# Paired attention heads on half of TensorE's rows and columns, in an attention and MLP kernel

## The chip, the cores and the metric

The kernel runs on one core of a Trainium2 chip. The metric is the device time of one execution in microseconds (us). Three runs of the kernel before took 725.65, 725.9 and 726.43 us; the median is 725.9. TensorE (PE in the profile) multiplies, VectorE (DVE), ScalarE (ACT) and GpSimd (POOL) work element by element, and SyncE (SP) issues most of the DMAs. TensorE reads its two operands from SBUF: a stationary one, which a weight load (PEld) brings into the array, and a moving one that streams through it. It writes to PSUM, which has eight banks.

## The reference

Attention with a sliding window and sink columns feeds a two-layer network with the gate h cos(h):

```python
scores = q @ k.T / sqrt(64)               # 4 batches, 8 heads, 768 positions, 64 per head
keep   = (pos_k < n_sink) | (0 <= pos_q - pos_k < window)      # n_sink 4, window 128
a      = softmax(where(keep, scores, -1e9))
x      = (a @ v), heads side by side      # 3072 tokens x 512
h      = x @ w_in                         # 512 x 2048
out    = (h * cos(h)) @ w_out             # 2048 x 512
```

The weights arrive as 64-bit floats and the result is float32. Most products are formed from numbers split into a rounded high part and a rest: high by high, high by rest, rest by high.

## The kernel before

The tokens are cut into 12 chunks of 256 (two 128-row blocks, CB = 2). Chunks 0 to 3 are the first 256 positions of the four batches; their heads are called early (`o.early`). The other eight chunks hold the late heads, whose queries see a band of one block and the sink columns. There are 8 heads in a chunk, so 32 early and 64 late heads, and `g` counts them.

An early head works in plain float32, which TensorE runs as two passes (two matmul records for each product). Query and key of two heads are loaded side by side and transposed on TensorE (`pe_turn`, L950), so that head 0 lies on rows 0 to 63 and head 1 on rows 64 to 127. `q_out` (L961) copies the query out of PSUM in two 64-row copies into `env.tqe`, where the other 64 rows of each head's 256 columns are zero; the key is copied whole. `scores_pe` (L987) is then one product over all 128 rows per head and query block, in which the zeros remove the other head. Likewise `load_v` (L921) puts a head's values beside 64 columns of zeros, and `values_pe` (L1204) forms one product per key block over all 128 columns, so that the second head of a pair adds to the bank of the first.

A late head splits query and key. The query of a pair is loaded and transposed once; each head has its rounded part and its rest stacked on the two row halves of one tile (`q_hi`, `q_lo`, L1004 and L1011). Each head loads its key twice, once on each row half (`load_k`, L908), transposes it on VectorE (`k_turn`), appends the sink columns, rounds it (`k_hi`) and subtracts (`k_lo`). `scores` (L1042) is two products of 264 columns per query block over 128 rows. VectorE merges the two halves of the window (`pick`), adds the mask and takes the minimum (`mask`); ScalarE takes the exponential; the probabilities are normalised, transposed on TensorE (`turn`), split, and `values` (L1220) forms seven products per head.

The dense work goes by pairs of chunks (512 tokens): six pairs of 16 slots. A slot is 12 products for h (`h_pair`, L476) and 12 for the output (`out_pair`, L523), each 128x128 by 512 columns. Dense pair 0 (chunks 0 and 1) runs beside the heads of chunks 2 and 3 and of the first late chunk, and so on; the last pair has no heads beside it. PSUM is shared out by name: in the late part four banks hold the outputs, two hold h, and attention has the two banks "s" and "tp".

The order on each engine is fixed when the kernel is built. `Plan.add` takes each step with its engines, an estimated duration, what it needs and a priority; `Plan.order` runs the list through a small model of the engines and emits the steps in the order in which they start there. The table `C` holds the offsets of these priorities. A step with several engines goes to one of them; `sub` offers POOL or DVE for subtractions. A step that issues DMAs is on SP's queue. `fill` (L1552) adds products that compute nothing, at the lowest priority, for moments when TensorE would wait in the model. `setup` (L233) comes ahead of the planned steps: it loads n_sink, window and the first two weight pieces (512 KB each) from ACT's queue. The first query and key loads are planned steps on SP's queue.

Of the kernel before, what the change touches and what calls it, by code (L numbers as in the profile page):

```python
# [31 lines left out]
    "POOLF": 0.999, "POOLPEN": 2.492, "R": 2, "RAW": 2, "SAME": 0.056, "SEM": 0.352, "SPE": -0.019, "STEP": 7.601,  # L32
# [140 lines left out]
def attn_moe_kernel(ctx, tc, q, k, v, n_sink, window, w_in, w_out, out):  # L173
# [59 lines left out]
    def setup():  # L233

        nc.scalar.dma_start(out=nw_i[:, 0, :], in_=n_sink.unsqueeze(0))
        nc.scalar.dma_start(out=nw_i[:, 1, :], in_=window.unsqueeze(0))
        nc.gpsimd.memset(ident, 0.0)
# [8 lines left out]
        for raw, src in env.first:  # L246
            nc.scalar.dma_start(out=raw.rearrange("p n w -> p (n w)"), in_=src)
# [104 lines left out]
    def x_minus(y, p, cs):  # L352
        def fn(e):
            nc.tensor.matmul(
                out=y.f(p, cs), lhsT=minus, rhs=xhi[:, p, cs], start=False, stop=True, skip_group_check=True
            )
        return fn

    def x_lo(y, p, cs, early):
        def fn(e):  # L360
            if early:
                copy(e, xlo[:, p, cs], y.f(p, cs))
            else:
                e.tensor_tensor(out=xlo[:, p, cs], in0=y.f(p, cs), in1=f32(xhi)[:, p, cs], op=ALU.subtract)
        return fn
# [195 lines left out]
    def sub(n):  # L561
        return (("POOL", 0.16 + n * 2.08e-3), ("DVE", dve(n)))
# [257 lines left out]
    def banded_path(ctx2):  # L820
# [634 lines left out]
        def after_softmax(g, o):  # L1455
# [76 lines left out]
            if o.sj:  # L1532
                oe = o.lead
                deps += oe.sinks
# [346 lines left out]
```

## Time and profile before

| | |
|---|---|
| median of three runs | 725.9 us (725.65 to 726.43) |
| profiled execution | 727.14 us, of which the span is 725.3 |
| PE busy | 707.8 us (98%) |
| PEld busy | 583.6 us (80%) |
| DVE busy | 599.3 us (83%) |
| ACT busy | 527.3 us (73%) |
| POOL busy | 127.0 us (18%) |
| granted TensorE clock, mean | 0.998 of full speed |
| DMA | 77.11 MB, mean 106 GB/s |

The span runs from the first to the last instruction of the core. Matmuls are pipelined and the profile models their ends, so records of neighbouring products overlap, and the time that a product costs is the distance to the start of the next. A wait is put down to whatever ended it last.

### The profile page before, as it was taken

How to read it: one execution, taken by the hardware profiler on the slowest of the kernel's cores; microseconds unless marked ns; L12 is line 12 of the kernel's file. 1: busy time of each engine (PE TensorE's matmuls, PEld its weight loads, DVE VectorE, ACT ScalarE, POOL GpSimd, SP SyncE). 2: the span in 40 equal slices, each digit the busy share in tenths (PEclk: the TensorE clock that was granted, in tenths of full speed). 3: DMA queues.
4: the chain of work that ended last, by engine and by line, in shares of the span. 5: the costliest groups of instructions: out<-in, count | busy, mean ns of one | idle time of the engine just before them, and what ended most of it. 6: DMA issues, size and time to landing. Idle time of an engine off the chain costs nothing.

```text
span 725.3 us, 12983 instructions
## 1 busy us (share of the span) xinstructions
PE 707.8 (98%) x3674; PEld 583.6 (80%) x3674; DVE 599.3 (83%) x1850; ACT 527.3 (73%) x1344; POOL 127.0 (18%) x213
## 2 busy tenths in 40 slices
PE   7888999999999999999999999999999999999997
PEld 6766787888888888888888888888888888888885
DVE  6889999998988978988978989888988875567763
ACT  3796886787797697796686886877887856566652
POOL 1010000000333222232231232232122322100000
PEclk9999999999999999999999999999999999999999
DMA  5665565533255333355433254533244410375651
GB/s 144 177 181 162 140 178 148 155 67 66 63 118 130 86 67 54 64 125 128 93 58 59 42 144 101 122 63 62 44 124 107 111 35 12 96 198 158 167 138 63
DMA packets 236500, 77.11 MB, mean 106 GB/s; under 512 B 221060, under 2 KB 221060, under 8 KB 236420
## 3 DMA queue, kind: packets, MB, share of 16 engines
q1 hardware_dynamic: 236128, 75.15, 43.5%
q10 hardware_dynamic: 292, 1.05, 0.5%
q8 instruction: 31, 0.51, 0.3%
q14 instruction: 49, 0.40, 0.2%
HBM read 69.86 MB, written 6.29 MB: 105 GB/s over the span
## 4 chain that ended last, share of the span: by engine, by line
PE 78%; ACT 12%; DVE 5%; issue 2%; DMA 2%; SPq 0%; ACTq 0%; DVEq 0%
PE h L476 30%; PE acc L523 30%; PE av L1239 4%; PE s L1048 4%; ACT p L1079 3%; PE s L992 2%; PE tp L1160 2%; PE av L1215 2%; DMA xk<-in_k_dram 2%; ACT p L1097 1%; ACT L485 1%; ACT L1079 1%; PE qk L955 1%; PE tp L1170 1%; ACT early L390 1%
## 5 line engine op out<-in xcount | busy, mean ns | idle before, releaser
L523 PE MATMUL acc<-whi_out,ghi 128*128 128x512 f32 x376 | 158.7, 422 | 0.0
L476 PE MATMUL h<-xhi,whi_in 128*128 128x512 f32 x384 | 155.3, 405 | 0.0
L476 PE MATMUL h<-xlo,whi_in 128*128 128x512 f32 x384 | 150.9, 393 | 0.0
L476 PE MATMUL h<-xhi,wlo_in 128*128 128x512 f32 x384 | 150.1, 391 | 0.0
L523 PE MATMUL acc<-whi_out,glo 128*128 128x512 f32 x376 | 147.8, 393 | 0.0
L523 PE MATMUL acc<-wlo_out,ghi 128*128 128x512 f32 x376 | 147.1, 391 | 0.0
L1198 POOL TENSOR_SCALAR_AFFINE_SELECT ph<-ph 128x512 fp32r<-128x512 f32 x128 | 87.2, 681 | 230.9 <-DVE ph L1191 227.1
L485 ACT ACTIVATE r<-h 128x512 f32<-128x512 f32 x96 | 57.1, 598 | 47.9 <-PE h L476 45.3
L476 PEld LDWEIGHTS h<-xlo,whi_in 128*128 128x128 f32 x384 | 72.1, 188 | 16.2
L523 PEld LDWEIGHTS acc<-whi_out,glo 128*128 128x128 f32 x376 | 70.6, 188 | 15.8
L476 PEld LDWEIGHTS h<-xhi,whi_in 128*128 128x128 f32 x384 | 72.3, 188 | 12.0 <-DVE r L498 0.3
L476 PEld LDWEIGHTS h<-xhi,wlo_in 128*128 128x128 f32 x384 | 72.5, 189 | 11.3
L523 PEld LDWEIGHTS acc<-whi_out,ghi 128*128 128x128 f32 x376 | 71.4, 190 | 10.4
L1079 ACT ACTIVATE p<-p,st 128x136 f32<-128x136 f32 (+1 forms) x192 | 79.3, 415 | 0.3
L523 PEld LDWEIGHTS acc<-wlo_out,ghi 128*128 128x128 f32 x376 | 71.3, 190 | 9.2
L498 DVE SCALAR_TENSOR_TENSOR r<-r,h 128x512 f32<-128x512 f32 x96 | 64.5, 674 | 16.9 <-ACT r L491 16.3
L507 ACT CAST ghi<-r 128x512 fp32r<-128x512 f32 x94 | 58.2, 619 | 19.6 <-PE acc L523 12.7
L514 DVE TENSOR_TENSOR glo<-r,ghi 128x512 fp32r<-128x512 f32 x94 | 65.3, 694 | 5.6 <-ACT ghi L507 4.9
L1070 DVE CUSTOM_DVE_ANT_0 p<-s,mk 128x136 f32<-128x136 f32 (+1 forms) x192 | 59.7, 313 | 6.2 <-PE s L992 2.8
L1008 ACT CAST l<-tq 64x256 fp32r<-64x256 f32 x64 | 25.8, 403 | 46.9 <-PE s L1048 46.4
L1056 DVE COPY_PREDICATED s<-mk,s 128x128 f32<-128x128 int32 x128 | 37.2, 291 | 25.6 <-PE s L1048 23.7
L1048 PEld LDWEIGHTS s<-r,l 128*128 128x128 f32 x256 | 46.4, 188 | 12.3 <-DVE ph L1191 1.4
(161 smaller groups left out, 1314.7 us busy)
## 6 DMA issues: line engine op xcount, KB each, us to landing
xk<-in_k_dram SPq DMA_DIRECT2D x256, 48.0 KB
raw<-in_moe_w_out_dram SPq DMA_DIRECT2D x16, 512.0 KB
wt<-in_moe_w_in_dram SPq DMA_DIRECT2D x32, 256.0 KB
raw<-in_moe_w_in_dram SPq DMA_DIRECT2D x14, 512.0 KB
v<-in_v_dram SPq DMA_DIRECT2D x64, 96.0 KB
raw<-in_v_dram SPq DMA_DIRECT2D x32, 192.0 KB
out_dram<-wt SPq DMA_DIRECT2D x22, 256.0 KB
wt<-in_moe_w_out_dram SPq DMA_DIRECT2D x20, 256.0 KB
```

Of the source, the lines that this page charges most:

```text
L476: nc.tensor.matmul(out=o.h, lhsT=w[:, c, fs], rhs=xx[:, c, :], start=(c == 0 and n == 0), stop=(c == NC - 1 and n == 2),)
L485: nc.scalar.activation(out=o.r, in_=o.h, func=AF.Sin, scale=0.5)
L498: nc.vector.scalar_tensor_tensor(out=o.r, in0=o.r, scalar=0.5, in1=o.h, op0=ALU.subtract, op1=ALU.mult)
L507: nc.scalar.copy(out=o.ghi, in_=o.r)
L514: e.tensor_tensor(out=o.glo, in0=o.r, in1=f32(o.ghi), op=ALU.subtract)
L523: nc.tensor.matmul(out=y.acc[j], lhsT=gg[:, j * P : (j + 1) * P], rhs=w[:, f, :], start=(f == 0 and n == 0), stop=(f == NFT - 1 and n == 2),)
L1048: nc.tensor.matmul(out=o.s_ps[j][:, :w], lhsT=o.l[:, j * P : (j + 1) * P], rhs=r.rearrange("p n s -> p (n s)")[:, c0 : c0 + w], start=(n = ...
L1056: nc.vector.copy_predicated(out=o.s_ps[j][:, :P], mask=below.bitcast(I32), data=o.s_ps[j][:, SW : SW + P])
L1070: nc.vector.tensor_tensor_reduce(out=o.pj[j][:, :w], in0=o.s_ps[j][:, :w], in1=masks[min(o.i0 + j, 2)][:, :w], op0=ALU.add, op1=ALU.min, s ...
L1079: nc.scalar.activation(out=o.pj[j][:, :w], in_=o.pj[j][:, :w], func=AF.Exp, bias=o.lead.st[:, 0, o.nth, j : j + 1], scale=-1.0, accum_out= ...
L1198: nc.gpsimd.affine_select(out=ph[:, :, b, :], in_=f32(ph)[:, :, 1, :], pattern=[[0, 2 * CB], [(-1, 1)[b], P]], compare_op=(ALU.is_gt, ALU. ...
L1239: nc.tensor.matmul(out=dst, lhsT=lhs, rhs=rhs, start=(n == 0), stop=(n == len(seq) - 1), skip_group_check=True)
```

## The change

Late heads are prepared in pairs. Key of head 0 is loaded on rows 0 to 63 and of head 1 on rows 64 to 127, query likewise; one rounding and one subtraction then serve both heads, for query and for key. `scores_two` forms the scores of both heads for one query block: for each head three products on its 64 rows (rounded by rounded, query rest by rounded key, rounded query by key rest), the two heads in turn, into banks "s" and "tp". `after_softmax` of the heads ahead is placed between the two score calls.

Early heads are prepared in pairs as well: no zeros, one copy of the query, scores as products on 64 rows, values as products of 64 columns into the two partition halves of one bank. The split of x after the early heads loses its product with the negated identity (`x_minus`), and its subtraction is on DVE. Query and key tiles of the early heads are double-buffered.

The first query and key loads move into `setup`: n_sink and the query on SP's queue, window and the key on ACT's queue, then one weight piece on each. The last output tile is copied in one step on ACT instead of two halves on ACT and DVE. `sub` no longer offers POOL for more than 256 columns. There are 110 fillers in place of 60 and 3 warming steps in place of 5, and the other numbers of `C` change.

```diff
-    "DV": 0.57, "DX": 4.638, "FILL": 60, "CV": 1.947, "CL": 15.777, "HO": -18.522, "SX": -5.15, "CR": 9.813,
+    "DV": -6.352, "DX": -1.287, "FILL": 110, "CV": 12.468, "CL": 26.528, "HO": -19.975, "SX": -6.773, "CR": 9.41,
-    "T": 6.724, "TH": 7.177, "WARM": 5, "WARM2": 0, "P0": 12.442, "A0": -3.102, "D0": 9.766, "G0": 3.059,
+    "T": 6.626, "TH": 6.919, "WARM": 3, "WARM2": 0, "P0": 9.866, "A0": 2.375, "D0": 8.59, "G0": -7.384, "S0": -8.12,
...
-        nc.scalar.dma_start(out=nw_i[:, 0, :], in_=n_sink.unsqueeze(0))
+        nc.sync.dma_start(out=nw_i[:, 0, :], in_=n_sink.unsqueeze(0))
         nc.scalar.dma_start(out=nw_i[:, 1, :], in_=window.unsqueeze(0))
+        for e, load in zip((nc.sync, nc.scalar), env.boot):
+            load(e)
...
-        for raw, src in env.first:
-            nc.scalar.dma_start(out=raw.rearrange("p n w -> p (n w)"), in_=src)
+        for e, (raw, src) in zip((nc.scalar, nc.sync), env.first):
+            e.dma_start(out=raw.rearrange("p n w -> p (n w)"), in_=src)
...
-        m = add([("PE", 0.12)], x_minus(y, p, cs), [i], t + 0.3)
-        env.minus.users.append(m)
-        j = add([("ACT", act(NT, False)), ("DVE", dve(NT))], x_lo(y, p, cs, True), [m], t + 0.6)
+        j = add([("DVE", dve(NT))], x_lo(y, p, cs), [i], t + 0.6)
...
-        return (("POOL", 0.16 + n * 2.08e-3), ("DVE", dve(n)))
+        return (("POOL", 0.16 + n * 2.08e-3), ("DVE", dve(n)))[n > NT :]
...
-            elif j < NJ - 1:
+            else:
                 i = [add(c[:1], out_scaled(y, j, other), d, c0 + 10.0)]
-            else:
-                i = [add([(e, w / 2)], out_half(y, j, n), d, c0 + 10.0) for n, (e, w) in enumerate(c)]
...
         def load_k(o):
-                for dup in range(2):
+                for h in range(2):
                     for c in range(2):
                         nc.sync.dma_start(
-                            out=o.xk[dup * 64 + c * 32 : dup * 64 + c * 32 + 32],
-                            in_=k[o.b, o.h, o.kb0 * P : (o.kb0 + o.nkb) * P, c * 32 : c * 32 + 32].rearrange(
+                            out=o.xk[h * 64 + c * 32 : h * 64 + c * 32 + 32],
+                            in_=k[o.b, o.h + h, o.kb0 * P : (o.kb0 + o.nkb) * P, c * 32 : c * 32 + 32].rearrange(
...
-        def q_out(o, odd):
-                r = slice(odd * 64, odd * 64 + 64)
-                copy(e, env.tqe[r, odd], o.qk[r, 0])
+        def q_out(o):
+                o.tq = env.tqe[o.btq.nth]
+                copy(e, o.tq, o.qk[:, 0])
...
+        def scores_pe(pair):
+                for j in range(CB):
+                    for o in pair:
+                        r = slice(o.odd * 64, o.odd * 64 + 64)
+                        c0 = max(o.i0 + j - 1 - o.kb0, 0) * o.sw
+                        nc.tensor.matmul(
+                            out=o.s_ps[j], lhsT=oe.tq[r, j * P : (j + 1) * P],
+                            rhs=oe.tk.rearrange("p n s -> p (n s)")[r, c0 : c0 + o.ws[j]], start=True, stop=True,
+                        )
...
+        def q_hi(o):
+                nc.scalar.copy(out=o.l, in_=o.tq)
+        def q_lo(o):
+                nc.vector.tensor_tensor(out=o.ql, in0=o.tq, in1=f32(o.l), op=ALU.subtract)
...
+        def scores_two(pair, j):
+                w, c0 = oe.ws[j], max(oe.i0 + j - 1 - oe.kb0, 0) * oe.sw
+                for o in pair:
+                    o.s_ps[j] = ps.tile([P, BW], F32, name=f"s_{o.tag}_{j}", tag=("s", "tp")[o.odd])
+                for n, (l, r) in enumerate(((oe.l, oe.r1), (oe.ql, oe.r1), (oe.l, oe.r2))):
+                    for o in pair:
+                        rows = slice(o.odd * 64, o.odd * 64 + 64)
+                        nc.tensor.matmul(
+                            out=o.s_ps[j][:, :w], lhsT=l[rows, j * P : (j + 1) * P],
+                            rhs=r.rearrange("p n s -> p (n s)")[rows, c0 : c0 + w], start=(n == 0), stop=(n == 2),
+                        )
...
+        def values_pair(pair, x):
+                av = x.f[oe.pair] = ps.tile([P, NT], F32, name=f"av_{oe.tag}", tag=oe.av_tag)
+                for n, (kb, qs) in enumerate(oe.cols):
+                    for o in pair:
+                        nc.tensor.matmul(
+                            out=av[o.odd * 64 : o.odd * 64 + 64, (qs[0] - oe.i0) * P : (qs[-1] + 1 - oe.i0) * P],
+                            lhsT=oe.v32[:, kb - oe.kb0, o.odd], rhs=o.pt[:, oe.offs[n] * P : oe.offs[n + 1] * P],
+                            start=(n == 0), stop=(n == len(oe.cols) - 1), skip_group_check=True,
+                        )
...
+        def score_two(g, j):
+            bss = [buf(tag, 1) for tag in ("s", "tp")]
+            c0 = add([("PE", 0.36)], scores_two(pair, j), [*oe.kr, *bss], te - 5 * T + C["DS"] + (3.25, 5.55)[j])
...
+            for n, w in enumerate(pair):
+                c1 = add([("DVE", dve(P) + 0.02)], pick(w, j), [c0], te - 5 * T + C["DS"] + (3.4, 5.7)[j] + 0.5 * n)
+                c2 = add(
+                    [("DVE", dve(w.w[j]) + 0.02)], mask(w, j),
...
+            else:
+                for j in range(CB):
+                    if behind and behind[0][1].comb:
+                        after_softmax(*behind.pop(0), (g, j))
+                    else:
+                        score_two(g, j)
```

## Rows read from the trace of the kernel before

**Rows 1.** The page's part 1, whole span: busy us, share, instructions.

```profile
PE 707.8 (98%) x3674; PEld 583.6 (80%) x3674; DVE 599.3 (83%) x1850; ACT 527.3 (73%) x1344; POOL 127.0 (18%) x213
```

**Rows 2.** Busy us by stretch: length, PE, PEld, DVE, ACT, POOL, clock, DMA.

```profile
0.00:57.00 57.00, 47.81 (x273) 39.31 (x274) 45.30 (x162) 38.95 (x129) 5.94 (x17) 1.00 0.62 165
20.00:57.00 37.00, 32.30 (x187) 24.98 (x187) 31.04 (x108) 33.05 (x113) 3.43 (x4) 1.00 0.65 171
57.00:190.00 133.00, 130.79 (x651) 105.41 (x652) 122.78 (x341) 101.34 (x248) 5.19 (x11) 1.00 0.49 124
190.00:640.00 450.00, 448.75 (x2396) 373.61 (x2395) 377.61 (x1215) 341.13 (x879) 115.84 (x186) 1.00 0.39 86
```

**Rows 3.** PE's groups by shape, whole span: busy us, mean ns, idle before.

```profile
L1239 PE MATMUL av<-ph,vr 128*64 128x128 f32 x128 | 28.8, 225 | 0.0
...
L1239 PE MATMUL av<-ph,vr 128*64 128x256 f32 x64 | 18.0, 281 | 0.0
...
L1556 PE MATMUL idle<-gt 128*128 128x256 f32 x60 | 13.1, 345 | 0.0
```

**Rows 4.** PE in order of time, late stretch: start us, us, instruction, count.

```profile
250.05 0.28 PE L1239 MATMUL av<-ph,vr 128*128 128x256 f32 x1
...
250.64 0.44 PE L523 MATMUL acc<-whi_out,ghi 128*128 128x512 f32 x1
250.92 0.40 PE L523 MATMUL acc<-wlo_out,ghi 128*128 128x512 f32 x1
...
260.56 0.41 PE L1048 MATMUL s<-r,l 128*128 128x264 f32 x2
260.80 0.39 PE L476 MATMUL h<-xhi,whi_in 128*128 128x512 f32 x1
```

**Rows 5.** PE in order of time, early heads beside dense products.

```profile
95.19 0.38 PE L992 MATMUL s<-tk,early 128*128 128x128 f32 x2
95.41 0.82 PE L1215 MATMUL av<-early,vpe 128*128 128x256 f32 x4
...
96.30 0.40 PE L476 MATMUL h<-xhi,wlo_in 128*128 128x512 f32 x1
96.53 0.39 PE L476 MATMUL h<-xlo,whi_in 128*128 128x512 f32 x1
...
97.45 0.59 PE L992 MATMUL s<-tk,early 128*128 128x256 f32 x2
97.88 0.38 PE L1170 MATMUL tp<-ident,p 128*128 128x128 f32 x2
```

**Rows 6.** DVE's groups by shape, 190 to 640 us.

```profile
L1039 DVE TENSOR_TENSOR r<-tk,r 128x408 fp32r<-128x408 f32 x57 | 34.0, 597 | 0.5
...
L1021 DVE STREAM_TRANSPOSE tk<-xk 128x384 f32<-128x384 f32 x57 | 32.1, 562 | 0.2
...
L1015 DVE TENSOR_TENSOR l<-tq,l 64x256 fp32r<-64x256 f32 x57 | 23.9, 420 | 1.5
```

**Rows 7.** The chain of waits, 0 to 70 us: start us, us, what.

```profile
2.32 5.88 DMA xk<-in_k_dram
...
8.34 0.66 PE qk L955 x2
```

**Rows 8.** All engines in order of time, the start.

```profile
4.70 0.69 PE L955 MATMUL qk<-ident,xq 128*128 128x128 f32 x2 [0.25 <-DVE neg L269]
```

**Rows 9.** Groups by line, 0 to 57 us.

```profile
L390 ACT COPY early<-qk 64x256 f32<-64x256 f32 x12 | 4.4, 366 | 12.2 <-PE qk L955 11.9
```

**Rows 10.** PE in order of time, the first dense product.

```profile
57.08 0.48 PE L476 MATMUL h<-xhi,whi_in 128*128 128x512 f32 x1
```

**Rows 11.** All engines in order of time, the end.

```profile
719.16 0.60 ACT L533 ACTIVATE raw<-acc 128x512 f32<-128x512 f32 x1 [0.76 <-PE acc L523]
...
720.51 0.38 ACT L543 ACTIVATE raw<-acc 128x256 f32<-128x256 f32 x1 [0.76 <-PE acc L523]
721.01 0.42 DVE L545 TENSOR_SCALAR raw<-acc 128x256 f32<-128x256 f32 x1 [6.60 <-ACT raw L543]
```

More of the change, by code (lines that the diff above doesn't have):

```diff
@@ L1025, in fn @@
             def fn(e):
-                sk = first.ts[:, o.h].unsqueeze(1).broadcast_to([P, o.nkb, NSINK])
-                copy(e, o.tk[:, :, P:], sk)
+                for h in range(2):
+                    r = slice(h * 64, h * 64 + 64)
+                    copy(e, o.tk[r, :, P:], first.ts[r, o.h + h].unsqueeze(1).broadcast_to([64, o.nkb, NSINK]))
             return fn
@@ L1362, in before_softmax @@
-                    i = add(dma(2), load_natural(xk_t, src, o.nkb), [bx], pk, lat=2.4 if g else 1.9)
+                        [("ACT", act(NT, False)), ("DVE", dve(NT))], q_out(o), [i, o.btq] + (early[:2] if g == 0 else []),
+                        t - 6 * T + C["EQ"] + 0.6,
+                    )
+                    bb.users.append(q0)
+                    bx, o.btk = buf("xk", 1), buf("tke", 2)
+                    src = lambda c: k[o.b, o.h + c, o.kb0 * P : (o.kb0 + o.nkb) * P, :]
+                    load = load_natural(xk_t, src, o.nkb)
@@ L1439, in softmax @@
+            for n, (_, o) in enumerate(group):
+                o.nm = [
+                    add(
+                        [("ACT", act(o.w[j]) + (0.0 if o.early else 0.19))], expo(o, j), ready, t + 1.02 * n + 0.01 * j,
+                        table="exp",
+                    )
+                    for j in range(CB)
+                ]
+                ex += o.nm
             t += 1.02 * (len(group) - 1) + 0.5
@@ new lines, in after_softmax @@
+            if o.early:
+                if o.odd == 0:
+                    return
+                pair = oe, _ = heads[g - 1], o
+                te = head_time(g - 1)
+                oe.bxv, bpt = buf("ve", 2), buf("phi", 1)
+                hold = [early[2:], [early_end]][g // 2] if g < 4 else []
+                v0 = add(dma(2), load_v_pair(oe), [oe.bxv, *hold], te - 2 * T + C["EV"] + 3.2, lat=2.4)
+                ready = [v0]
+                for m, w in enumerate(pair):
+                    pt = buf(w.tp_tag, 1)
+                    p0 = add([("PE", 0.107 * o.n)], turn_early(w), w.nm + [pt], head_time(g - 1 + m) + C["EA"] + 1.3)
+                    w.bp.users.append(p0)
+                    both = [("ACT", act(o.n * P, False)), ("DVE", dve(o.n * P))]
+                    p1 = add(both, p_out(w), [p0, ready[1] if m else bpt], head_time(g - 1 + m) + C["EA"] + 1.8)
+                    pt.users.append(p1)
+                    ready.append(p1)
+                bav = buf(oe.av_tag, 1)
+                y0 = add([("PE", 0.84)], values_pair(pair, x), [*ready, bav], te + C["EA"] + 5.0)
+                for bb in (oe.bxv, bpt, *early[2:]):
+                    bb.users.append(y0)
@@ L1640, in banded_path @@
             waiting.append((g, o))
-            if behind:
-                after_softmax(*behind.pop(0))
+            if o.early:
+                if behind and o.odd:
+                    for _ in range(2):
+                        after_softmax(*behind.pop(0))
+            elif o.odd == 0:
+                while behind and behind[0][1].early and len(behind) > 2 - g % 4:
+                    after_softmax(*behind.pop(0))
+            else:
+                for j in range(CB):
+                    if behind and behind[0][1].comb:
+                        after_softmax(*behind.pop(0), (g, j))
+                    else:
+                        score_two(g, j)
             if len(waiting) == o.nq:
```

361 lines of the change are left out of this document (140 added, 221 removed), and 11 rows, old and new, of the table C.

## The prediction

> **What bounds the kernel now.** I read the totals first, then the stretches, then the order of work on TensorE inside two stretches, and last the chain at the start and the end. The totals show PE busy 98% of the span, DVE 83%, ACT 73% [rows 1]. A busy PE counts the pipeline's latency too, so the share alone proves little. The stretches do: from 57 to 190 us and from 190 to 640 us PE has 130.79 of 133 and 448.75 of 450 us, at a granted clock of 1.00 (the 2.4 GHz level) throughout, while DVE falls from 122.78 of 133 to 377.61 of 450 [rows 2]. So after about 60 us the time is PE's list of products, and an instruction taken off that list is taken off the span, as long as DVE (92% in 57 to 190 us) keeps up. Before 57 us PE is not full (47.81 of 57, and 60 of its products there are fillers that compute nothing, 13.1 us [rows 2, 3]): this is a chain that runs through DMA, PE, ACT and DVE in turn, with ACT at 33.05 and DVE at 31.04 of the 37 us from 20 to 57 [rows 2].
>
> What a product costs is read from starts, not durations, since a dense 128x512 product is recorded as 0.40 us and the next one starts 0.23 to 0.24 us later [rows 4, 5]. A late score (one head, one 128-query block, two products of 264 columns) takes 260.80 - 260.56 = 0.24 us. A late value block of seven products takes from 250.05 to the second dense product after it, 250.92, less one dense step of 0.23, so 0.64 us [rows 4]. In the early heads a score of 128 columns takes 95.41 - 95.19 = 0.22 us, one of 256 takes 97.88 - 97.45 = 0.43, and the values of one head take 96.30 - 95.41 less 0.23 = 0.66 us [rows 5]. An early pair of heads so costs PE 2 x (0.22 + 0.43 + 0.66) = 2.62 us in scores and values; its transposes are the same before and after.
>
> **The change, part by part.** The sum is made against the profiled execution, 727.1 us (725.3 of span and 1.8 around it). That is 1.2 above the median of 725.9, which I take off at the end.
>
> *Late scores.* Per pair of heads and query block two calls of 0.24 us go (0.48), and one call comes with six products of 264 columns on 64 rows each, ordered low rows, high rows, low, high. The trace has no product on half of the rows, so I bound it. One product of 264 columns takes 0.12. If the two row halves run side by side completely, the call is three steps, 0.36; if not at all, six steps, 0.72. There are 32 pairs x 2 blocks = 64 calls, so the term lies between 64 x (0.36 - 0.48) = -7.7 and 64 x (0.72 - 0.48) = +15.4 us. I take 0.40, a third of a step above the low end, because each step must now hide two weight loads where the score row hides one per 0.12 us: 64 x -0.08 = -5.1 us. All 64 calls lie in the stretches where PE is full, so this counts whole.
>
> The Trainium skill, TensorE: Matmul & The Clock Gate, Part 3, gives 3.07 times for four row tiles and 2.38 times for three column tiles, some 78% of ideal; an estimate for two tiles by that page is 1.56 times, 0.46 us a call, and this term would be -1.3 us. No row here tests it.
>
> *Early pairs.* Scores become four products on row halves, values become products of 64 columns into the two halves of one bank. Complete overlap halves 2.62 us: -1.31 a pair; no overlap: 0. The weight loads have more time here (0.11 us for 128 columns of each of the two passes, [rows 5]), so I take -1.31 on PE. Eight of the 16 pairs (chunks 2 and 3) run beside the first dense pair, mostly in 57 to 190 us: -10.5 us if nothing else binds. DVE has 122.78 of 133 us there [rows 2]. Squeezed by 10.5 that would be 100%, so DVE has to lose work too. It does: a late pair loses one key transpose, one key rest and one query rest (0.562, 0.597 and 0.420 us [rows 6]), and of these operations 57 of the 64 that 64 heads need fall in 190 to 640 us, so seven, 3.5 pairs, are prepared before 190: 5.5 us, and merged copies give about one more. About 116 of 122.5 us is 95%, tighter than the 92% of now; I give back 2 us for that: -8.5.
>
> *The prologue.* The other eight pairs run before 57 us. There the first key transposes start at 8.34 us, released by a key load that took 5.88 us [rows 7], beside the two weight loads that ACT's queue issues at the start. Query and key now go out ahead of the weights, key on ACT's queue behind one tiny load, query on SP's behind the other; one weight load follows each. On SP the first value loads wait behind two small issues and one weight issue, and the first values are needed only after a whole softmax. PE took the query at 4.70 us [rows 8]; if the key is there once those two transposes are done, at about 5.0, 3.3 us go. Bounds: 0 (the masks or the weights are late next) to -3.6 (both at 4.70). I take -3.3. Per pair, at least the second of two 64-partition copies goes, 0.37 us of ACT or DVE time [rows 9], and at most PE's 1.31: between -3.0 and -10.5 us over eight pairs. Since the chain passes through all engines and ACT and DVE are at 89% and 84% from 20 to 57 us [rows 2], I take -4.0. The extra fillers, 50 of 256 columns, some 0.12 us each by the score row, come last in priority; at worst each stands once before needed work, +6 us; I take 0, because they run where PE would wait.
>
> *Late preparation.* Key load, transpose, rounding, rest, and query rounding and rest are now once a pair. In 190 to 640 us that takes (34.0 + 32.1 + 23.9) / 2 = 45 us from DVE [rows 6], and ACT loses the roundings. Neither is the bound there, so 0 on the span; it lowers the risk of PE waiting. Half of the key DMAs go as well; the queues were hidden. What is added is a wait: a paired score needs both attention banks, and behind it on PE stand dense products. A call holds each bank for PE's 0.4 and some four DVE steps of 0.3, about 2 us, and with values and transposes a bank is held for about 8 us of a pair's 14 to 15, so I cost it at 0; if each call waited 0.1 us it would be 6.4.
>
> *The end.* The last copy was halved over ACT and DVE, but the DVE half began only at 721.01, after ACT's 720.51 + 0.38; together 0.92 us. One ACT copy of 512 columns took 0.60 [rows 11]: -0.3.
>
> Sum: -5.1 - 8.5 - 3.3 - 4.0 - 0.3 = -21.2; 727.1 - 21.2 = 705.9, and 704.7 on the median's footing. I say 705.
>
> **Rivals.** *First, the tile change drains TensorE (slower).* A product's record outlasts its step by 0.40 - 0.23 = 0.17 us; if PE empties whenever it goes from whole-array to half-array products and back, every call pays up to 0.34. That is 64 late calls, +21.8, and 16 early calls in the full stretch, +5.4, and in the prologue perhaps +2: 705 + 29 = 734. It decides from 21 / 160 = 0.13 us per change. Against it: the late value block has three products of 64 columns among four of 128, and its 0.64 us is what 1280 streamed columns take at the dense rate of 512 per 0.23, plus 0.06 [rows 3, 4]. So if 64-column products are a mode of their own, a change costs next to nothing; if they are not, the row says nothing.
>
> The Trainium skill, TensorEngine Tiling (Array Packing), Key Properties, says that changing the tiling mode drains the engine; this is that rival, and the value block, as far as it goes, does not agree.
>
> *Second, the halves do not overlap (slower).* Late +15.4, early 0, start -3.3, copies -1, end -0.3: 737. For it: no row shows two products on the array at once. Against it: nothing in the operands forbids it, as the halves write separate banks or separate partitions.
>
> *Third, the order loses what PE gains.* DVE or the shared banks become the bound from 57 us on; only the start, half of the late term and a third of the early term stay: -3.3 - 2.5 - 3.5 = -9, so 717. For it: DVE's 92% in 57 to 190 us. Against it: the work that DVE loses.
>
> **How the numbers follow.** The forecast has 0.66, with its own range of 693 to 712 (late term at -7.7 and prologue at -10.5 below; early term and prologue at half above). The lossy order has 0.12 (712 to 723), the drain 0.12 (centred on 734, but reaching down to 715 at smaller prices), no overlap 0.10. A range of 692 to 724 leaves out no overlap, most of the drain and little else, about 2 in 10. Within 0.2% means within 1.5 us, about what a measurement can tell from no change: 0.03. Slower takes no overlap and some of the drain: 0.15. Faster 0.82.
>
> **What would show it.** Right: pairs of half-row products whose starts lie a few ns apart, and a late call of 0.36 to 0.45 us from its first product to the next dense one; early scores and values of a pair in 0.65 us each; the first key transpose near 5 us; the first dense product before 52 us instead of 57.08 [rows 10]; PE still 98% full after it. Wrong: products of the six starting 0.11 us apart one by one (no overlap); a gap of over 0.1 us ahead of the first half-row product or the first dense one behind it (drain); DVE at 97% and PE with idle time released by DVE in 50 to 170 us (lossy order).

## The result, and the profile after

The changed kernel takes 734.19 us (733.23 to 736.97, four runs) beside 725.77 us (724.52 to 726.43) for the kernel before on the same chip: a ratio of 1.0124, 95% interval 1.0091 to 1.0157, so 8.4 us slower where 705 us and faster were forecast. The profiled execution is the slowest of the four, 736.97 us, with a span of 735.2. In two stretches of it the granted clock fell (0.79 of full in 12 to 20 us and in 64 to 72 us); in the executions at 733 us the mean clock was 0.999 against 0.993 in this one. e2 below, which differs only in the order of the six late products, had the full clock there, and its row in the table shows the start and pair 0 without the fall.

The page's totals, and the busy time by stretch (length, PE, PEld, DVE, ACT, POOL, clock, DMA share, GB/s), answer to [rows 1, 2]:

```profile
PE 714.6 (97%) x3840; PEld 558.9 (76%) x3840; DVE 565.8 (77%) x1823; ACT 493.3 (67%) x1221; POOL 106.5 (14%) x158
```

```profile
57.00:190.00 133.00, 129.88 (x684) 96.05 (x684) 118.58 (x323) 100.18 (x238) 10.40 (x15) 0.99 0.46 124
190.00:640.00 450.00, 448.63 (x2441) 356.00 (x2440) 346.33 (x1202) 304.15 (x763) 91.41 (x126) 1.00 0.30 70
```

All other engines have less to do, and PE is as full as before. From 190 to 640 us DVE lost 31 us and ACT 37, and PE waited no more. So the loss is in PE's own list. Where it is, the start of the first `h` product of each pair of dense chunks shows (PE in order of time, us; the last column is the rest of the span behind the last `acc` product). e2, e8 and e16 are experiments told below.

| | first | pair 0 | pair 1 | pair 2 | pair 3 | pair 4 | last pair | tail |
|---|---|---|---|---|---|---|---|---|
| before | 57.1 | 124.6 | 107.2 | 112.2 | 112.2 | 110.4 | 96.8 | 4.8 |
| after | 50.3 | 123.4 | 111.4 | 115.0 | 116.3 | 113.1 | 100.1 | 5.6 |
| e2 | 48.5 | 121.6 | 111.6 | 115.1 | 116.4 | 113.2 | 100.0 | 5.9 |
| e8 | 47.7 | 120.0 | 107.3 | 110.4 | 111.7 | 109.3 | 99.4 | 4.7 |
| e16 | 48.2 | 120.5 | 115.8 | 115.9 | 113.4 | 113.1 | 97.5 | 4.7 |

The start gave 6.8 us, pair 0 another 1.2; pairs 1 to 4, where 59 of the 64 late score calls run, took 13.9 more, the last pair 3.2 and the tail 0.8: +9.9. One late score call in that stretch (PE in order of time: start us, us, instruction, count), and the weight loads beside it:

```profile
270.64 0.39 PE L467 MATMUL h<-xlo,whi_in 128*128 128x512 f32 x1
270.95 0.39 PE L1036 MATMUL s<-r,l 64*128 64x264 f32 x2
271.18 0.29 PE L1036 MATMUL s<-r,ql 64*128 64x264 f32 x2
271.30 0.28 PE L1036 MATMUL s<-r,l 64*128 64x264 f32 x2
271.52 0.50 PE L467 MATMUL h<-xhi,whi_in 128*128 128x512 f32 x1
271.85 0.39 PE L467 MATMUL h<-xhi,wlo_in 128*128 128x512 f32 x1
```

```profile
270.95 0.19 PEld L1036 LDWEIGHTS s<-r,l 64*128 64x128 f32 x2 [0.35 <-issue]
271.06 0.19 PEld L1036 LDWEIGHTS s<-r,ql 64*128 64x128 f32 x2
...
271.51 0.19 PEld L467 LDWEIGHTS h<-xhi,whi_in 128*128 128x128 f32 x1
```

The two halves do run side by side: each row holds two products (3 to 4 ns apart in the trace), and the six take three steps. But from 270.64 to 271.85, less two dense steps of 0.23, the call costs 0.75 us, and three steps of 0.12 are 0.36 of that. The other 0.39 lies in four late steps. The first half products come 0.31 us after the dense one instead of 0.23, the second pair of halves comes 0.23 after the first instead of 0.12, and behind the last pair the next dense products come after 0.22 instead of 0.12 and after 0.33 instead of 0.23. The weights of the first half products (270.95) and of the first dense product behind them (271.51) are loaded in the same moment in which these products start, where those of the second pair are loaded 0.12 us ahead (271.06). A pair cost 0.48 before [rows 4]; at 0.75, 64 calls are +17.3 us. The call shown is typical: the median of the 54 calls with no other wait is 0.75 too.

The early calls beside dense products, which answer to [rows 5]:

```profile
91.61 0.40 PE L514 MATMUL acc<-whi_out,glo 128*128 128x512 f32 x1
91.94 0.87 PE L1194 MATMUL av<-early,early 128*64 128x256 f32 x8
92.74 0.50 PE L514 MATMUL acc<-whi_out,ghi 128*128 128x512 f32 x1
93.08 0.40 PE L514 MATMUL acc<-wlo_out,ghi 128*128 128x512 f32 x1
...
97.63 0.40 PE L467 MATMUL h<-xlo,whi_in 128*128 128x512 f32 x1
97.96 0.93 PE L977 MATMUL s<-early,early 64*128 64x128 f32 x8
98.81 0.50 PE L514 MATMUL acc<-whi_out,ghi 128*128 128x512 f32 x1
99.15 0.39 PE L514 MATMUL acc<-wlo_out,ghi 128*128 128x512 f32 x1
```

Less two dense steps, the values cost 1.01 us a pair and the scores 1.06: 2.07, where the single heads cost 2.62 and 1.31 was forecast. The first half product is late here too, 0.33 us behind the dense one. The 0.33 to 0.34 between the two dense products behind is no sign of the halves: behind early values over all 128 columns it is 0.32 (e14 below).

The start, which answers to [rows 7, 8, 10]: the first key transposes, the first dense product, and, by DVE's order of time, its first unpacking of a weight:

```profile
4.98 0.63 PE L948 MATMUL qk<-ident,xk 128*128 128x128 f32 x2
...
50.26 0.50 PE L467 MATMUL h<-xhi,whi_in 128*128 128x512 f32 x1 [0.65 <-DVE xlo L357]
```

```profile
9.43 0.43 DVE L576 TENSOR_SCALAR wt<-raw 128x512 int32<-128x512 int32 x1 [4.61 <-DMA raw<-in_moe_w_in_dram]
```

The keys come 3.4 us sooner and the dense work 6.8 (8.6 in e2, at the full clock), but DVE now stands 4.61 us for the weights, which are unpacked ahead of the masks.

### The profile page after: what moved, and what is told of

It is laid out like the page before. It is cut to its first block, busy times and chain, and to the rows that moved or that the text cites. A ratio compares the mean times of both kernels' runs of the same rounds, so it can differ in the third digit from the quotient of the medians.

```text
span 735.2 us, 12798 instructions
## 1 busy us (share of the span) xinstructions
PE 714.6 (97%) x3840; PEld 558.9 (76%) x3840; DVE 565.8 (77%) x1823; ACT 493.3 (67%) x1221; POOL 106.5 (14%) x158
## 4 chain that ended last, share of the span: by engine, by line
PE 82%; ACT 6%; DMA 5%; DVE 4%; issue 1%; SPq 0%; ACTq 0%; POOL 0%; POOLq 0%
PE acc L514 33%; PE h L467 32%; PE av L1220 5%; PE s L1036 5%; ACT p L1067 2%; DMA raw<-in_v_dram 2%; PE tp L1147 2%; DMA raw<-in_moe_w_out_dram 1%; PE av L1194 1%; PE tp L1156 1%; PE s L977 1%; DMA raw<-in_moe_w_in_dram 1%; ACT early L381 1%; DVE raw L1238 1%; PE idle L1544 1%
## 5 line engine op out<-in xcount | busy, mean ns | idle before, releaser
L467 PE MATMUL h<-xhi,whi_in 128*128 128x512 f32 x384 | 160.4, 418 | 2.1 <-DVE r L489 1.5
L1181 POOL TENSOR_SCALAR_AFFINE_SELECT ph<-ph 128x512 fp32r<-128x512 f32 x128 | 94.9, 741 | 367.4 <-DVE ph L1174 363.0
L514 PEld LDWEIGHTS acc<-whi_out,glo 128*128 128x128 f32 x376 | 70.6, 188 | 17.3 <-DVE glo L505 1.4
L505 DVE TENSOR_TENSOR glo<-r,ghi 128x512 fp32r<-128x512 f32 x94 | 67.2, 715 | 7.3 <-ACT ghi L498 5.5
L1058 DVE CUSTOM_DVE_ANT_0 p<-s,mk 128x136 f32<-128x136 f32 (+1 forms) x192 | 54.5, 312 | 2.9 <-PE s L977 2.3
L1095 ACT CAST vr<-v 128x192 fp32r<-128x192 f32 x64 | 22.5, 351 | 42.5 <-PE av L1220 40.7
L1220 PE MATMUL av<-ph,vr 128*128 128x128 f32 (+3 forms) x384 | 49.0, 244 | 0.0
L1220 PEld LDWEIGHTS av<-ph,vr 128*128 128x128 f32 (+1 forms) x384 | 43.4, 161 | 3.9 <-issue 1.1
```

The source lines that it names most:

```text
L467: nc.tensor.matmul(out=o.h, lhsT=w[:, c, fs], rhs=xx[:, c, :], start=(c == 0 and n == 0), stop=(c == NC - 1 and n == 2),)
L505: e.tensor_tensor(out=o.glo, in0=o.r, in1=f32(o.ghi), op=ALU.subtract)
L514: nc.tensor.matmul(out=y.acc[j], lhsT=gg[:, j * P : (j + 1) * P], rhs=w[:, f, :], start=(f == 0 and n == 0), stop=(f == NFT - 1 and n == 2),)
L1058: nc.vector.tensor_tensor_reduce(out=o.pj[j][:, :w], in0=o.s_ps[j][:, :w], in1=masks[min(o.i0 + j, 2)][:, :w], op0=ALU.add, op1=ALU.min, s ...
L1095: nc.scalar.copy(out=o.vr[:, :, 0, :], in_=o.v32)
L1181: nc.gpsimd.affine_select(out=ph[:, :, b, :], in_=f32(ph)[:, :, 1, :], pattern=[[0, 2 * CB], [(-1, 1)[b], P]], compare_op=(ALU.is_gt, ALU. ...
```

## The experiments

The theory after the result: PE pays about 0.20 us for every change between products on the whole array and products on halves, whatever the halves compute. The rivals: the order of the six products or their number of weight loads costs it; or the pairing's order and waits do. The kernel before was timed beside each run, and the ratios are against it.

**The price of a change by itself (e4 to e7).** To the kernel before, one product of 16 columns is added ahead of each late head's transposes, 64 in all, into a bank made 16 columns wider.

```diff
                     o.tp = late_bank(o, 0)
+                    nc.tensor.matmul(
+                        out=o.tp[0:128, NT : NT + 16], lhsT=whi_in[0:128, 1, 512:640], rhs=whi_in[0:128, 2, 512:528],
+                        start=True, stop=True,
+                    )
```

That is e4. In e5 `lhsT` and `rhs` are rows 0:64 and nothing else differs. In e6 and e7 `lhsT` is 64 columns wide, 512:576, and `out` is partitions 0:64 or 64:128; both operands are also read as plain fp32, so that these two differ from e4 by a second pass and the number format as well.

> The kernel before with one more product of 16 columns ahead of the two transposes of each late head (64 in all), over all 128 rows and 128 columns, into unused columns of the same bank: the control. Theory A and its rivals alike: one weight load and a product of minimal length, 0.06 to 0.12 us each, 4 to 8 us, about 732 us.

> The same added product on rows 0 to 63 alone, all else as in the control. Theory A: it goes into half-row shape and back each time, 0.2 us each way, so 64 x 0.4 = 25 us over the kernel before and about 20 over the control, 750 us. If a change of shape costs nothing and only a pair of halves has a price: as the control, about 732 us.

> The same added product with 128 rows and 64 stationary columns into PSUM partitions 0 to 63, in plain float32 (two passes). The late value block has 64-column products of this placement and no gap around them. If 64 columns at the low end are not a shape of their own: as the control plus one more pass, about 734 us. If they are, and the value block hides it otherwise: about 750 us.

> As the one before, into PSUM partitions 64 to 127. Theory A in its column form (the early value pairs showed 0.2 us on each side): about 750 us. If columns never need a change of shape: about 734 us.

Measured: e4 728.26 us (ratio 1.0035, 1.0022 to 1.0047), e5 744.57 (1.0261, 1.0219 to 1.0303), e6 745.18 (1.027), e7 744.38 (1.0259). The same product costs 0.04 us a call on the whole array and about 0.25 more on half of the rows: (744.57 - 728.26) / 64 = 0.255. Plain products of 64 columns, low or high, come out at the same 0.25 over e4. PE in order of time in e4 and in e5:

```profile
250.49 0.39 PE L523 MATMUL acc<-whi_out,glo 128*128 128x512 f32 x1
250.72 0.17 PE L1159 MATMUL tp<-whi_in 128*128 128x16 f32 x1
250.75 0.42 PE L1164 MATMUL tp<-ident,p 128*128 128x128 f32 x2
...
251.23 0.40 PE L523 MATMUL acc<-wlo_out,ghi 128*128 128x512 f32 x1
```

```profile
252.04 0.40 PE L523 MATMUL acc<-whi_out,glo 128*128 128x512 f32 x1
252.37 0.27 PE L1159 MATMUL tp<-whi_in 64*128 64x16 f32 x1
252.57 0.44 PE L1164 MATMUL tp<-ident,p 128*128 128x128 f32 x2
...
253.08 0.40 PE L523 MATMUL acc<-wlo_out,ghi 128*128 128x512 f32 x1
```

From one dense product to the second behind the call it is 1.04 us against 0.74. The half product comes 0.33 behind the dense one instead of 0.23, and the transposes 0.20 behind it instead of 0.03. With as many products and weight loads in e5 as in e4, neither their number nor the score's operands, order or waits are the cause: the change of shape itself costs, on the way in and on the way out. All four runs came in under their expectations, e4 by 3.7 us and the others by about 5, and theory A's size doesn't hold for them: 16 us over the control are 0.13 us a change, not 0.20. The price of a change isn't one number; the late call has one late step more, between its first two pairs of halves.

**The order of the six products (e2).** All three of the low rows, then all three of the high rows.

```diff
-                for n, (l, r) in enumerate(((oe.l, oe.r1), (oe.ql, oe.r1), (oe.l, oe.r2))):
-                    for o in pair:
+                for o in pair:
+                    for n, (l, r) in enumerate(((oe.l, oe.r1), (oe.ql, oe.r1), (oe.l, oe.r2))):
```

> The changed kernel with the six products of a paired late score ordered by head (three on the low rows, then three on the high rows) in place of by turns. The number of changes of tile shape stays. If the halves overlap completely when they take turns (theory A, and B too), three steps of 0.113 us are added to each of 64 calls: +22 us, about 756 us, a call of 1.09 us. If they never overlapped (theory C: the loss is missing overlap, not the change of shape), the order makes no difference: 734 us.

Measured: 735.33 us in two runs (ratio 1.0135, 1.0108 to 1.0163), no different from the changed kernel. The order of time:

```profile
261.87 0.39 PE L1036 MATMUL s<-r,l 64*128 64x264 f32 x2
262.10 0.29 PE L1036 MATMUL s<-r,ql 64*128 64x264 f32 x2
262.22 0.29 PE L1036 MATMUL s<-r,l 64*128 64x264 f32 x2
262.44 0.50 PE L514 MATMUL acc<-whi_out,ghi 128*128 128x512 f32 x1
```

My expectation failed, and the rows say why: the fourth product in the program starts 10 ns after the first, beside it, and so in 63 of the 64 calls. In these two orders the overlap is the same, and the order is no cause of the loss.

**The change of shape taken out of the changed kernel (e8, e14).** e8: three products on all 128 rows for the six, which leaves out that the two heads are kept apart.

```diff
-                for n, (l, r) in enumerate(((oe.l, oe.r1), (oe.ql, oe.r1), (oe.l, oe.r2))):
-                    for o in pair:
-                        rows = slice(o.odd * 64, o.odd * 64 + 64)
+                for l, r, o, first, last in (
+                    (oe.l, oe.r1, pair[0], True, False),
+                    (oe.ql, oe.r1, pair[1], True, True),
+                    (oe.l, oe.r2, pair[0], False, True),
+                ):
```

> The changed kernel, with each late call's six 64-row products replaced by three products over all 128 rows (two into the even head's bank, one into the odd head's), so that it computes other scores than wanted; loads, preparation, order, waits and the number of bytes stay. Theory A (two changes of tile shape a call, 0.20 us each, are the loss): a call falls from 0.76 us to 3 x 0.12 = 0.36 to 0.40, 64 calls give back 64 x 0.36 to 0.40 = 23 to 26 us, so 707 to 711 us, and a middle dense pair takes about 109 us instead of 115. Rival B (the pairing's order, its waits for VectorE or its shared buffers are the loss): the call gets shorter, the wait moves, and the time stays above 729 us.

Measured: 714.61 us (712.29 to 714.84; ratio 0.9844, 0.9829 to 0.986). 19.6 us come back, and the kernel is faster than before. The call in order of time:

```profile
256.28 0.39 PE L467 MATMUL h<-xlo,whi_in 128*128 128x512 f32 x1
256.50 0.28 PE L1038 MATMUL s<-r,l 128*128 128x264 f32 x1
256.63 0.28 PE L1038 MATMUL s<-r,ql 128*128 128x264 f32 x1
256.75 0.29 PE L1038 MATMUL s<-r,l 128*128 128x264 f32 x1
256.87 0.40 PE L514 MATMUL acc<-whi_out,ghi 128*128 128x512 f32 x1
257.11 0.40 PE L514 MATMUL acc<-wlo_out,ghi 128*128 128x512 f32 x1
```

257.11 - 256.28 less 0.46 is 0.37, and the same three steps stand without the 0.39. With the order, the waits and the preparation unchanged, rival B falls. That e8 also has half as many products and weight loads is no second explanation, by e5 against e4. It came 4 us short of the 23 to 26 expected, with middle pairs of 107 to 112 us; why wasn't tested. Some of it is waits that come back: PE's waits in pairs 1 to 4 are 1.6 us in e8 and 0.6 in the changed kernel.

e14 takes the changes out of the early values too; it leaves out one head of the pair at each key block.

```diff
-                    for o in pair:
+                    o = pair[n % 2]
...
-                            out=av[o.odd * 64 : o.odd * 64 + 64, (qs[0] - oe.i0) * P : (qs[-1] + 1 - oe.i0) * P],
-                            lhsT=oe.v32[:, kb - oe.kb0, o.odd], rhs=o.pt[:, oe.offs[n] * P : oe.offs[n + 1] * P],
+                        out=av[:, (qs[0] - oe.i0) * P : (qs[-1] + 1 - oe.i0) * P],
+                        lhsT=oe.v32[:, kb - oe.kb0].rearrange("p a d -> p (a d)"),
```

> As e8, and each early pair's value products over all 128 columns with one product where two stood, so that it computes other values than wanted. Theory A (the two changes of shape cost the early value calls too, 0.20 us each): such a call falls from 1.01 us to 0.55 to 0.60, 8 calls beside the dense products give 3.3 to 3.7 us, the 8 ahead of them between nothing and as much: 707.5 to 711.5 us against e8's 714.6. Rival B (the early calls are bound by their columns, or by what feeds them): 714 us or more.

Measured: 714.03 us (712.05 to 714.45), the same as e8: the time is rival B's. The call is shorter as theory A had it:

```profile
86.21 0.40 PE L514 MATMUL acc<-whi_out,glo 128*128 128x512 f32 x1
86.44 0.82 PE L1196 MATMUL av<-early,early 128*128 128x256 f32 x4
87.01 0.48 PE L514 MATMUL acc<-whi_out,ghi 128*128 128x512 f32 x1
87.33 0.39 PE L514 MATMUL acc<-wlo_out,ghi 128*128 128x512 f32 x1
```

1.12 - 0.46 = 0.66 us instead of 1.01, and pair 0 took 118.2 instead of 120.0; but the last pair took 1.2 more. So the price is there in the early calls, and what it is worth to the whole isn't settled by this run. Both sides of this comparison are plain fp32, so in plain fp32 it is the 64 columns that cost 0.35 us a call, not the number format.

**The start (e3, e9, e13).** e3 is the kernel before with the first q and k loads issued ahead of the weights; e9 is the same with the planner told the old times, so that the order stays.

```diff
+        for e, load in zip((nc.sync, nc.scalar), env.boot):
+            load(e)
...
-        for raw, src in env.first:
-            nc.scalar.dma_start(out=raw.rearrange("p n w -> p (n w)"), in_=src)
+        for e, (raw, src) in zip((nc.scalar, nc.sync), env.first):
+            e.dma_start(out=raw.rearrange("p n w -> p (n w)"), in_=src)
```

> The kernel before with one part of the change: n_sink and the first query on SP's queue, window and the first key on ACT's queue, ahead of the two weight pieces. By the prediction's step the start moves 3.3 us earlier and the time falls to about 722.5 us. If the first heads' softmax or the weights are late next, the first dense product stays at 57 us and the time at 725.8.

> The kernel before, with the first q and k loads issued ahead of the weights as in the change, and with the planner told the old times, so that every other instruction keeps the old order. Theory A (the start step of the prediction): the first key transposes go 3.3 us sooner and the rest follows: 722.5 us, 721.0 at best. Rival B (the next thing in the prologue is as late as the loads were, VectorE's masks that free the score banks): 725.5 to 726 us, no change. The loss of 11 us in the earlier run with the loads first came from the planner's other order in both theories, and does not come back here.

Measured: e3 736.76 us (ratio 1.0172, 1.0141 to 1.0202), e9 728.85 (1.0038, 1.0024 to 1.0052). Both theories missed: the loads alone make it slower by 3 us even in the old order. In e9 the first dense product starts at 60.0 instead of 57.1. DVE's and PE's order of time there:

```profile
8.73 0.43 DVE L597 TENSOR_SCALAR wt<-raw 128x512 int32<-128x512 int32 x1 [3.05 <-DMA raw<-in_moe_w_in_dram]
```

```profile
13.55 0.76 PE L1001 MATMUL s<-tk,early 128*128 128x128 f32 x2 [4.46 <-DVE st L1079]
```

The wait for the keys is gone, and PE waits 4.46 us for DVE instead, whose masks stand behind weights that now come later. That is only a third of the loss. PE had stood idle from 9.1 to 13.55 us, and from 11.5 to 18.4 us its granted clock was at the lower level (0.5 of full, 1.2 GHz), where before it stayed at full. The stretch from 10 to 20 us in e9 and in the kernel before (length, PE, PEld, DVE, ACT, POOL, clock, DMA share, GB/s):

```profile
10.00:20.00 10.00, 6.37 (x31) 5.91 (x32) 7.37 (x23) 3.37 (x11) 0.00 (x0) 0.66 0.27 74
```

```profile
10.00:20.00 10.00, 9.92 (x67) 9.32 (x66) 8.09 (x28) 3.47 (x13) 0.38 (x1) 1.00 0.55 150
```

The scores that start at 13.55 started at 12.42 in the kernel before, so the wait cost 1.1 us; the key transposes that stood at 15.01 start at 18.17, and the lag is then 3.2. The other executions of e9 have mean clocks of 0.993 to 0.997, against 0.998 to 1.000 for the kernel before, which points to such a stretch in them too. The other 8 us of e3 came with its other order, 6 of them in pair 2, far from the start (118.2 us instead of 112.2).

e13 is the changed kernel with these loads as before.

```diff
-        for e, load in zip((nc.sync, nc.scalar), env.boot):
+        for e, load in zip((nc.sync, nc.sync), env.boot):
...
-        for e, (raw, src) in zip((nc.scalar, nc.sync), env.first):
-            e.dma_start(out=raw.rearrange("p n w -> p (n w)"), in_=src)
+        for raw, src in env.first:
+            nc.scalar.dma_start(out=raw.rearrange("p n w -> p (n w)"), in_=src)
```

> The changed kernel with the first loads issued as in the kernel before (both weight pieces at once on ScalarE's queue, q and k on SyncE's), every other instruction in the changed order. Theory A (the start step of the prediction: 3.3 us from the early loads): the first dense product comes 3.3 us later, 736.5 us. Rival B (as in e9, the weights that VectorE unpacks ahead of the masks are as late as the keys were, and the early pairs alone brought the start forward): within 1 us of the changed kernel's 734.2, or up to 2.9 faster, 731.

Measured: 734.12 us (ratio 1.0118, 1.0102 to 1.0133), as the changed kernel. Its first key transposes start at 7.60 us, 2.6 later, and its first dense product at 49.2, against 48.5 in e2, whose loads are the changed kernel's and whose clock was full there as well. Rival B by the time: the early loads gave at most 0.7 us at the first dense product and nothing to the whole. The other 7.9 us of the start came with the early pairs, the fillers and the new order, which no run takes apart.

**Late heads one by one again (e1, e10 to e12, e15, e16).** In each the changed kernel has the single scores and the preparation by head of the kernel before; they differ in the planner's offsets, and so in the order. e1 has the late offsets of before; e10 and e11 have costs and offsets set anew; e12 has mostly the offsets of before; e15 and e16 also 60 fillers and the last step of the norms (`row_t`) planned earlier.

```diff
-            c0 = add([("PE", 0.36)], scores_two(pair, j), [*oe.kr, *bss], te - 5 * T + C["DS"] + (3.25, 5.55)[j])
+                c0 = add([("PE", 0.23)], scores(o, j), [o.ql, *o.kr, bs], t - 5 * T + C["DS"] + (3.25, 5.55)[j])
```

> Late heads as in the kernel before (each head prepared alone, scores as two products over 128 rows), all else of the change kept: early pairs, loads first, table C of the change but for the late heads' own offsets. Theory A (each change between whole-array and half-row products costs TensorE 0.2 us, so a paired score call takes 0.75 us where two single ones took 0.48): 64 x 0.27 = 17 us come back, about 717 us. Theory B (the halves' products are as cheap as forecast, 0.36 to 0.40 a call, and the loss is in the new order of the dense and last stages): taking the pairs away costs 5 us more, about 739 us.

> The changed kernel with its late heads one by one as in the kernel before (scores over all 128 rows), and the planner's offsets and TensorE costs set anew for that work, so that its order has few waits. Theory A (late pairing is the loss, early pairs and early loads the gain): 725.8 - 6.8 (first dense product sooner) - 1 to 5 (first dense pair) = 714 to 718 us. Rival B (what made the earlier run without late pairing slow, 744 us, lies in the early pairs or the loads): 730 us or more.

> As the run before, with other offsets of the planner (an order found apart from the first). It tells how far the order alone moves the time. Theory A: 714 to 718 us again, within 3 us of the run before. Rival B: the order decides more than the shape of the products does, and the two differ by over 8 us.

> As e10 (early pairs and early loads kept, late heads one by one over all 128 rows), with the planner's costs and most of its offsets as in the kernel before and only those of the early heads and of the start set anew. Theory A (the shape changes of the late pairs are the loss, and e1, e10 and e11 were slow by waits of their own order): 714 to 720 us, middle dense pairs at 112 us and next to no wait of TensorE for VectorE after the first pair. Rival B (early pairs cost the dense stretch more than they give): middle pairs above 114 us again and 728 us or more.

> As e12 (early pairs and early loads, late heads one by one), with at least 60 fillers at the start and the last check planned 8 us ahead of the end. Theory A (e12 lost by its halved clock at the start and its late check, and all four by waits of their orders): first dense product at 48 to 50 us, first dense pair 120 us, middle pairs 110 to 113, tail 5 us as before: 713 to 720 us. Rival B (single late heads beside early pairs cost the late stretch itself): middle pairs at 114 us and more in this order too, 728 us or more.

> As e15 in another order, planned apart from it. Theory A: 714 to 721 us. Rival B: 728 us or more. Where the two differ by over 5 us, it is the order that decides.

Measured: 744.22, 739.06, 734.05, 738.21, 736.85 and 731.57 us (e16: ratio 1.0082, 1.0064 to 1.01). None reached the 714 to 721 us expected; by the times alone the rivals' figures came true in e10, e12, e15 and e16 (e10 and e11 differ by 5.0 us, which is neither theory's). The start and pair 0 kept their gains (e16 in the table), and pairs 1 to 4 took 16 us more in e16 than in the kernel before. PE's waits in these pairs, the larger ones, in e16 and then all of them in the kernel before (what waits, for what: us in total, times, longest):

```profile
PE h L457 <- DVE r L479: 4.8, 2, 3.1
PE gp L1118 <- DVE gc L1105: 2.0, 4, 1.0
PE gp L1118 <- ACT r L472: 1.6, 2, 0.8
```

```profile
PE tp L1160 <- DVE st L1070: 0.9, 4, 0.2
```

With the smaller ones e16 has 9.9 us of waits there, and 3.4 us of pair 1 ran at the lower clock level. In e11, at the full clock throughout, waits are 5.4 of 16 us. So a good part of the 16 isn't explained by any wait that the trace records. In e12 the start also ran at a granted clock of 0.71 and 0.67 from 10 to 30 us, with 24 fillers. These pairs hold no early heads, so rival B of e12 and e15 (early pairs cost the late stretch themselves) would have to act through the order or the buffers; runs of the same late work differ by up to 12.7 us, so the order matters much. That isn't a proof: whether early pairs beside single late heads can be had faster than 725.8 us stays open, since none of my six orders keeps PE full there.

## Why the prediction was wrong

**The step that failed** is the late scores' term: "I take 0.40, a third of a step above the low end", 64 x -0.08 = -5.1 us. The halves do overlap wholly, as taken; what was left out of the 0.40 is the change of shape. The call costs 0.75 us and the term measures +17.3, 22 us off (by one call's cost; pairs 1 to 4 with 59 of the calls took 13.9 us more). The bounds of -7.7 to +15.4 didn't hold it, because they counted steps of products only and not what lies between two kinds of product. The first rival had this mechanism: 0.17 us a change, 734 us. Measured are 0.20 a change in the late calls, over three bare steps, and 734.19. Its late term fits, but that the total fits to 0.2 us is luck: early pairs and start came out some 3 us better than it had them, the last pair and the tail 4 worse. It had a chance of 0.12, and the range ended at 724, short of it. The sign given for it, one gap of over 0.1 us, is met only as a sum: the late steps are 0.08 to 0.11 us each. The rival was put so low on a row that can't speak of it: the late value block, whose 64-column products follow 128-column ones without a gap. In e6 and e7 64-column products do pay. Those are plain fp32 and the value block's are rounded fp32r. That this is the difference is a guess, and no run here has fp32r products of 64 columns in a place of their own. But the kernel before has eight fp32r products with a single stationary column (`cs`), each alone between dense ones, and none is late (PE in order of time):

```profile
651.98 0.39 PE L476 MATMUL h<-xlo,whi_in 128*128 128x512 f32 x1
652.21 0.28 PE L704 MATMUL cs<-col,one_r 128*1 128x256 f32 x1
652.33 0.39 PE L476 MATMUL h<-xhi,whi_in 128*128 128x512 f32 x1
652.56 0.39 PE L476 MATMUL h<-xhi,wlo_in 128*128 128x512 f32 x1
```

The steps are 0.23, 0.12 and 0.23 us, the plain ones of 512 and 256 columns. So fewer columns cost nothing in fp32r here, while half of the rows in fp32r (e5) and half of the columns in plain fp32 (e14 against e8) do. The prediction itself said that the row says nothing if these are no mode of their own, and then used it as evidence.

The Trainium skill, TensorEngine Tiling (Array Packing), Key Properties, says that changing the tiling mode drains the engine. e5 (0.25 us a call over e4) and e8 (0.38 us a call less) agree that a change costs; the narrow fp32r products don't show it.

**Early pairs**: -1.31 a pair was forecast and -0.55 measured, by two calls a pair that each cost 0.35 to 0.4 us more than half of the old. For the values e14 shows that this is the change of shape (0.66 us without it, just half of the old 1.32); for the scores it is taken over from there. For eight pairs -0.55 is -4.4, where -10.5 less 2 for DVE was forecast. In e8, without the late loss, pair 0 gained 4.6.

**Start and prologue**: -3.3 and -4.0, together -7.3; measured -6.8 with 3.4 us at the lower clock level, -8.6 (e2) and -9.4 (e8) at the full clock. The sum was near and the shares were wrong, so that it was near is luck. "The masks or the weights are late next" stood as the lower bound, 0, and e9 and e13 show that it was the case: loads 0.7 us at best, or worse than 0, and early pairs, fillers and order the rest.

**Late preparation** at 0, and the wait for two banks at 0: right. PE's only recorded waits in pairs 1 to 4 are 0.6 us for DVE. The three groups of [rows 6] fell by 44 us, as forecast; that DVE as a whole lost only 31 comes of other groups that grew (`r<-r` from 10.5 to 21.4 us, for one). But cheap work wasn't worthless: in the six runs that take it back PE waited for DVE again.

**The end**: -0.3 forecast, +0.8 in the tail, and the last pair took 3.2 us more, which no term had; of that 1.6 is PE's wait for DVE ahead of the sums of the columns (`cs`), absent before, and about 0.6 a late value block of seven products that now falls into it. Why the rest is there I didn't test.

**The other rivals.** No overlap, 737 us, came near the measured time by another way, and the pairs of starts rule it out. The lossy order, 717, didn't happen in the changed kernel; waits of its kind stand in e1, e3, e10 to e12, e15 and e16.

With the late change of shape away, the profiled execution of e8, the fastest of its four, took 712.3 us against the 705.9 of the sum: 4 us by the early pairs, 2 by the late pairs (-3.2 in pairs 1 to 4 instead of -5.1), 3 by the last pair and the tail, and the start 2 better. What keeps the median at 714.6 no trace shows.

## What to carry to other kernels

Count the changes of shape on TensorE before counting columns: a call on halves between whole-array products pays 0.25 to 0.4 us here, as much as two to three of its own steps of 0.12. The paired score saved one such step (three where two single heads took four) and paid 0.39 for it. By these numbers what should gain is a long run of halved products between two changes, or fewer calls that change at all; no run here is of a kernel built so. And a row that shows no cost for a neighbour of the new operation is no evidence until it is known that the neighbour is of the same kind; where a rival names a mechanism with a price near its deciding point, the range has to reach it.

## What the runs showed that I had not expected

- A product of 16 columns on half the array costs 0.3 us between whole-array products, and the same product on the whole array 0.04 (e5, e4). An fp32r product with one column costs no more than its own step.
- Products on the two row halves run side by side in both orders of issue tried: in e2 the program's fourth product starts 10 ns after its first. The Trainium skill, TensorE: Matmul & The Clock Gate, Part 3, has products start in program order, some 4 ns apart; the 3 to 4 ns agree with the changed kernel, the order doesn't with e2.
- Loads moved ahead can cost time through an engine that they do not feed: 3 us in e9, 1.1 by weights that came 2.2 us later to DVE, and the rest while the granted clock was at the lower level behind PE's wait.
